# Products of zeros that warm TensorE: 256 columns instead of 512, twice as many

## The chip, the core and the metric

The kernel runs on one core of a Trainium2 chip. The metric is the device time of one execution in microseconds; lower is better. The core has five engines with a queue of instructions each: PE (TensorE, matrix products, with its weight loads shown apart as PEld), DVE (VectorE), ACT (ScalarE), POOL (GpSimd) and SP (SyncE, which only issues transfers here). An engine takes its instructions in the order in which they were written and waits where an operand is not there yet.

## The reference

An attention layer whose keys and values are first mixed block by block with a balanced 8x8 matrix for each of 32 heads, and then a feed-forward layer with the gate h * cos(h). Batch 4, 8 heads, 768 positions, head width 64, 8 blocks of 96; model width 512, inner width 2048.

```python
P = sort_net
for _ in range(5):                                # the balancing
    P = P - np.max(P, axis=-1, keepdims=True)
    P = np.exp(P)
    P = P / (np.sum(P, axis=-1, keepdims=True) + 1e-09)
    P = P / (np.sum(P, axis=-2, keepdims=True) + 1e-09)
k_sorted = np.einsum('bhij,bhjcd->bhicd', P, k_b)
v_sorted = np.einsum('bhij,bhjcd->bhicd', P, v_b)
scores = scale * np.matmul(q_b, k_sb.transpose(0, 1, 2, 4, 3))
attn = softmax(scores)
x = attn @ v_sb                                   # heads side by side: 3072 x 512
h = x @ w_in
out = (h * np.cos(h)) @ w_out
```

## The kernel before

The whole order of work is written out by hand (`tc.manual_schedule()`: nothing is moved by a scheduler). The kernel has three parts.

**Head.** At the start a 128x128 tile `warm` is filled with zeros on DVE (L231), and `keep_warm` (L244 to L248) multiplies it by its own first column, repeated over `cols` columns. The result goes to a PSUM tile that nobody reads: such a product of zeros only keeps TensorE at work. 14 of them, 512 columns each, run while the first loads arrive.

**Balancing.** `rounds(it)`, called five times, does the balancing of all 32 matrices in 32 partitions: one exponential on ACT (L335) and six operations on DVE (`normalize`, L309 to L314) in each round, every one of them waiting for the one before. Beside this chain the other engines prepare: POOL clears tiles and issues loads, PE transposes the first queries (`q_twice`, L323, 16 transposes in each of four calls) and ACT places them in SBUF (`q_place`, L329). The PSUM tiles of `q_twice` come from a pool of two, so its third call must wait for the first `q_place`, its fourth for the second. Between these calls `idle(times)` puts more products of zeros on PE: 4 after the first two calls of `q_twice` in round 0, 2 after the third and 2 after the fourth, in round 3. `idle` calls `keep_warm` with 512 columns. PE's written order up to the end of the balancing is therefore: 14 products of zeros; `q_twice(0)`, `q_twice(1)`; 4 products of zeros; `q_twice(2)`; 2; `q_twice(3)`; 2; and then `block` (L386), which needs the finished balanced matrix `sorted_by` (written by DVE in L314), the picking matrix in `pair` and a PSUM tile that `q_place(2)` has left.

**The rest.** `block` spreads the balanced matrix over 128 partitions, `spread` (L393, DVE) masks it, `kp` and `ks` (L408) sort the keys with it, `v0` (L785) the values, and the scores (L804), the softmax and the feed-forward layer (up products L860 and L672, cosine L676, gate L680, down products L697 and L881) follow, in eight groups of 384 positions. There are other products of zeros in this part (`fill=` in `s_ps`, `v0`, `p_ps`, `av_products`), with 512 columns in some calls and 256 in others; they are given straight to `keep_warm`.

Of the kernel before, what the change touches and what calls it, by code (L numbers as in the profile page):

```python
# [10 lines left out]
FP32 = mybir.dt.float32  # L11
# [7 lines left out]
def kernel(  # L19
# [46 lines left out]
    big = ctx.enter_context(tc.tile_pool(name="big", bufs=3, space=bass.MemoryType.PSUM))  # L66
# [177 lines left out]
    def keep_warm(times, t, cols=512):  # L244
        for _ in range(times):
            nc.tensor.matmul(
                t[:, :cols], warm[:], warm[:, :1].to_broadcast([128, cols]),
                start=True, stop=True)  # L248

    keep_warm(14, big.tile([128, 512], FP32, name="idle", tag="big"))  # L250


    V, A = nc.vector, nc.scalar
# [75 lines left out]
        A.copy(dst[:, h2], turns.pop(h2).rearrange("d e i r p -> d e i (r p)"))  # L329

    def idle(times):
        keep_warm(times, big.tile([128, 512], FP32, name="idle", tag="big"))

    def rounds(it):
        nc.scalar.activation(E, less[:], AF.Exp)  # L335
        if it == 0:
            A.copy(
                order.rearrange("k (p r) -> k p r", r=QR),
                ident[:blk, :blk].rearrange("k (r p) -> k p r", r=QR))
            q_twice(0)  # L340
            q_twice(1)
            idle(4)
        if it == 3:
            q_place(0)
            q_twice(2)
            idle(2)
            q_place(1)
            q_twice(3)
            idle(2)
# [905 lines left out]
```

## Time and profile before

| what | value |
|---|---|
| time, median of 3 runs | 232.1 us (231.99 to 232.11) |
| the profiled execution's own time | 231.61 us |
| its span, first to last instruction | 229.8 us |
| so outside the span | 1.8 us |
| PE products in the span | 2245 |
| products of zeros on the tile `idle` that the trace recorded | 21 of 22, first at 1.0 us, last at 11.0 us |

A row of a timeline gives the start in us from the span's beginning, the length, the engine, the line, what is written and read, the shape and the count; in brackets how long the engine had been idle just before and what ended the idle time. The length of a row of several products reaches from the first start to the last end. Products are pipelined: one lasts longer than the distance from its start to the start of the next, and it is this distance, the spacing, that a row of products costs. It is (length of the row - length of one product) / (count - 1). A few products are missing from the trace, so counts are now and then one short.

### The profile page before, as it was taken

The numbers are of one execution on the slowest core, as the hardware profiler recorded it, in microseconds if no ns is written. First come the engines' busy times: TensorE is split into PE (matmuls) and PEld (weight loads), VectorE is DVE, ScalarE is ACT, GpSimd is POOL, SyncE is SP. The second block draws the span as 40 slices with busy tenths as digits, with TensorE's granted clock in tenths as the row PEclk, the third lists the DMA queues.
The fourth block names the chain that finished last, engine by engine and source line by source line (L and its number), as shares of the span: only waits on it lengthen the run. The fifth ranks groups of instructions, "written<-read, shape, count | busy, mean of one in ns | idle before, by whom it ended". The sixth has DMA issues, their size and how long they took to land.

```text
span 229.8 us, 5513 instructions
## 1 busy us (share of the span) xinstructions
PE 220.8 (96%) x2245; PEld 138.7 (60%) x2268; DVE 170.8 (74%) x291; ACT 154.4 (67%) x207; POOL 96.1 (42%) x121
## 2 busy tenths in 40 slices
PE   8788999999999999999999999999999999999994
PEld 3378898567765566655665456655655565556554
DVE  6769968978698778868489977987699769646700
ACT  5659877777889858797688466736674667716521
POOL 7999999399950197943609000800000000000000
PEclk9999999999999999999999999999999999999999
DMA  6999999994999799667979939964924440351012
GB/s 83 225 187 207 202 206 236 195 227 148 124 124 191 171 139 148 118 135 146 162 118 163 135 74 148 210 98 81 206 92 80 90 160 0 69 147 46 0 46 94
DMA packets 67833, 31.21 MB, mean 136 GB/s; under 512 B 56416, under 2 KB 63200, under 8 KB 67552
## 3 DMA queue, kind: packets, MB, share of 16 engines
q0 software_dynamic: 24048, 13.64, 43.3%
q1 hardware_dynamic: 43472, 17.02, 35.1%
q8 instruction: 18, 0.29, 0.5%
q10 hardware_dynamic: 288, 0.20, 0.3%
q14 instruction: 7, 0.06, 0.1%
HBM read 27.27 MB, written 6.29 MB: 146 GB/s over the span
## 4 chain that ended last, share of the span: by engine, by line
PE 90%; DVE 3%; POOL 2%; issue 1%; ACT 1%; POOLq 0%; ACTq 0%
PE h L672 32%; PE o L697 30%; PE h L860 5%; PE o L881 4%; PE av L628 4%; PE sc L441 3%; PE ks L408 2%; PE o L1219 2%; PE pps L838 1%; PE sc L507 1%; PE xps L659 1%; PE vs L785 1%; PE vs L452 1%; PE qps L268 1%; PE xps L847 1%
## 5 line engine op out<-in xcount | busy, mean ns | idle before, releaser
L672 PE MATMUL h<-xT,w_in_t 128*128 128x384 bf16 x448 | 78.4, 326 | 0.1
L697 PE MATMUL o<-w_out_t,gg 128*128 128x512 bf16 x303 | 73.7, 379 | 1.0 <-issue 0.3
L676 ACT ACTIVATE c<-h,half_pi 128x768 f32<-128x768 f32 x56 | 50.5, 902 | 26.0 <-PE h L672 25.0
L680 DVE TENSOR_TENSOR gg<-c,h 128x768 bf16<-128x768 f32 x56 | 52.7, 949 | 19.5 <-ACT c L676 19.5
L672 PEld LDWEIGHTS <-w_in_t 128*128 128x128 bf16 x448 | 42.2, 98 | 26.3 <-DVE xT L259 0.6
L697 PEld LDWEIGHTS <-gg 128*128 128x128 bf16 x320 | 29.0, 99 | 28.3
L573 ACT ACTIVATE p_buf<-s 96x768 bf16<-96x768 f32 x32 | 26.6, 843 | 5.2 <-DVE s L494 4.0
L179 POOL COPY vperm<-kv 64x768 bf16<-64x768 bf16 (+2 forms) x12 | 28.4, 2416 | 3.9 <-DMA kv<-in_v_dram 3.9
L494 DVE TENSOR_TENSOR s<-sc,mx 96x384 f32<-96x384 f32 (+1 forms) x33 | 24.3, 735 | 1.6
L492 DVE TENSOR_REDUCE mx<-sc 96x4 f32<-96x384 f32 (+1 forms) x33 | 24.0, 729 | 0.2 <-PE sc L507 0.2
L641 DVE TENSOR_TENSOR xn<-av,r 96x512 bf16<-96x512 f32 x32 | 22.0, 687 | 1.1
L129 POOL DMA_DIRECT2D kv<-in_q_dram x24 | 16.0, 676 | 0.7 <-issue 0.7
L257 ACT COPY kv<-o 128x512 f32<-128x512 f32 (+2 forms) x10 | 5.2, 524 | 14.1 <-PE o L697 11.5
L257 ACT CAST kTs<-ks 128x512 bf16<-128x512 f32 (+1 forms) x18 | 11.0, 630 | 5.3 <-PE ks L408 4.4
L639 DVE RECIPROCAL r<-av 96x8 f32<-96x8 f32 x32 | 6.4, 199 | 9.6 <-PE av L628 9.1
L129 POOL DMA_DIRECT2D q_mem<-in_q_dram x16 | 10.7, 687 | 2.0 <-DMA kv<-in_v_dram 1.5
L881 PE MATMUL o<-w_out_t,gg 128*128 128x512 bf16 x45 | 11.2, 379 | 0.2
L259 DVE COPY kv<-o 128x512 f32<-128x512 f32 (+1 forms) x5 | 3.1, 612 | 11.1 <-PE o L1219 8.5
L860 PE MATMUL h<-xT,w_in_t 128*128 128x192 bf16 x128 | 11.1, 246 | 0.0
L441 PE MATMUL sc<-kTs,q_turned 128*128 128x96 bf16 x152 | 11.1, 206 | 0.0
L599 POOL CAST held<-q_turned 96x1 f32<-96x1 bf16 x2 | 0.4, 184 | 24.3 <-DMA q_turned<-q_mem 16.3
L860 PEld LDWEIGHTS <-w_in_t 128*128 128x128 bf16 x128 | 10.5, 98 | 0.0
(134 smaller groups left out, 285.6 us busy)
## 6 DMA issues: line engine op xcount, KB each, us to landing
out_dram<-kv SPq DMA_DIRECT2D x12, 256.0 KB, 2.7
out_dram<-o_s SPq DMA_DIRECT2D x10, 256.0 KB, 3.5
w_in_t<-in_moe_w_in_dram POOLq DMA_DIRECT2D x4, 512.0 KB, 11.7
w_out_t<-in_moe_w_out_dram POOLq DMA_DIRECT2D x4, 512.0 KB, 12.3
kv<-in_k_dram POOLq DMA_DIRECT2D x2, 768.0 KB, 9.8
kv<-in_v_dram POOLq DMA_DIRECT2D x2, 768.0 KB, 12.9
pair<-in_k_dram POOLq DMA_DIRECT2D x2, 768.0 KB, 12.3
kv<-in_v_dram POOLq DMA_DIRECT2D x6, 256.0 KB, 5.3
```

The lines of the kernel that those rows point to most:

```text
L129: nc.gpsimd.dma_start(out=q_heads[:, i, :, e], in_=src[:, ih * IC + i, :, e])
L179: nc.gpsimd.tensor_copy(dst, src)
L492: nc.vector.reduce_max(mx[:], scv, axis=AX.X)
L494: nc.vector.tensor_tensor(s, scv, mx.to_broadcast(list(s.shape)), op=ALU.subtract)
L573: nc.scalar.activation(p[:, :, :blk], s_t.pop((n, u)).rearrange("p e h c -> p (e h) c"), AF.Exp, scale=scale)
L641: nc.vector.tensor_tensor(xn.rearrange("p h e d -> p e h d"), avv[:, :, :, :D], r.to_broadcast([blk, 2, H2, D]), op=ALU.mult)
L672: nc.tensor.matmul(h[:, f2, :w], w_in_t[:, kk, f * 128:(f + 1) * 128], xT[n][:, kk], start=(kk == 0), stop=(kk == KC - 1))
L676: nc.scalar.activation(c[:], h[:, :, :w], AF.Sin, bias=half_pi[:, 0:1])
L680: nc.vector.tensor_tensor(gt[n, fp // 2][:, f:f + 2], c[:], h[:, :, :w], op=ALU.mult)
L697: nc.tensor.matmul(o[:], gt[n, f // 4][:, f % 4, ts * 128:(ts + 1) * 128], w_out_t[:, f, :], start=(f == 0), stop=(f == FC - 1))
L860: nc.tensor.matmul(o[:, part, f2 * w:(f2 + 1) * w], w_in_t[:, kk, f * 128:(f + 1) * 128], xT[0][:, kk, h * w:(h + 1) * w], start=(kk == 0) ...
L881: nc.tensor.matmul(out_ps[ts][:], gt[0, q][:, f % 4, ts * 128:(ts + 1) * 128], w_out_t[:, f, :], start=(f == 0), stop=(f == FC - 1))
```

## The change

Two calls of `keep_warm` ask for 256 columns and for twice as many products: at the head 28 instead of 14, and in `idle` 8, 4 and 4 instead of 4, 2 and 2. The number of columns stays 7168 at the head and 4096 beside the balancing. The other calls of `keep_warm` stay as they are.

```diff
-    keep_warm(14, big.tile([128, 512], FP32, name="idle", tag="big"))
+    keep_warm(28, big.tile([128, 512], FP32, name="idle", tag="big"), 256)
...
     def idle(times):
-        keep_warm(times, big.tile([128, 512], FP32, name="idle", tag="big"))
+        keep_warm(2 * times, big.tile([128, 512], FP32, name="idle", tag="big"), 256)
```

Every product brings its own weight load. On PE the end of the head reads as follows before, with the last products of zeros ahead of the first transpose (`q_mem` holds the queries as loaded, `qps` their transposes):

```order
L246 LDWEIGHTS warm
L246 MATMUL idle<-warm 128x512
L246 LDWEIGHTS warm
L246 MATMUL idle<-warm 128x512
L323 LDWEIGHTS q_mem [waits DMASW0_49]
L323 MATMUL qps<-ident,q_mem 64x4x24 [waits Pool_49]
```

And now:

```order
L246 LDWEIGHTS warm
L246 MATMUL idle<-warm 128x256
L246 LDWEIGHTS warm
L246 MATMUL idle<-warm 128x256
L246 LDWEIGHTS warm
L246 MATMUL idle<-warm 128x256
L246 LDWEIGHTS warm
L246 MATMUL idle<-warm 128x256
L323 LDWEIGHTS q_mem [waits DMASW0_49]
L323 MATMUL qps<-ident,q_mem 64x4x24 [waits Pool_49]
```

Nothing was moved; the transpose still waits for the load of the queries alone, and stands 28 rows later in PE's order. The second place on PE is the end of the balancing, where the last call of `idle` stands ahead of `block` (`pair` is the picking matrix). Before:

```order
L246 LDWEIGHTS warm
L246 MATMUL idle<-warm 128x512
L246 LDWEIGHTS warm
L246 MATMUL idle<-warm 128x512
L386 LDWEIGHTS pair [waits DVE_49,Pool_49]
L386 MATMUL bl<-sorted_by,pair 128x8 [waits Activation_49]
```

And now:

```order
L246 LDWEIGHTS warm
L246 MATMUL idle<-warm 128x256
L246 LDWEIGHTS warm
L246 MATMUL idle<-warm 128x256
L246 LDWEIGHTS warm
L246 MATMUL idle<-warm 128x256
L246 LDWEIGHTS warm
L246 MATMUL idle<-warm 128x256
L386 LDWEIGHTS pair [waits DVE_49,Pool_49]
L386 MATMUL bl<-sorted_by,pair 128x8 [waits Activation_49]
```

`block` waits for the same three engines as before. From here on every instruction of PE stands 44 rows later (22 products and their 22 weight loads), 4582 rows in all instead of 4538. The orders of ACT and SP are the same word for word, and on DVE and POOL only numbers of tiles differ.

## The prediction

> **What bounds the kernel now.** I read the page first, then the chain of waits over the first 15 us, then PE's timeline and its weight loads over the same stretch, because all 22 products that the change touches lie between 1.0 and 11.4 us. The page's engine row and its row of shares of the chain that ended last:
>
> ```profile
> span 229.8 us, 5513 instructions
> ...
> PE 220.8 (96%) x2245; PEld 138.7 (60%) x2268; DVE 170.8 (74%) x291; ACT 154.4 (67%) x207; POOL 96.1 (42%) x121
> ...
> PE 90%; DVE 3%; POOL 2%; issue 1%; ACT 1%; POOLq 0%; ACTq 0%
> ```
>
> PE carries 90% of the chain over the whole kernel, so one could think that any product more or less on PE is felt. For the stage at hand that is not so. This is PE's timeline there:
>
> ```profile
> 1.00 5.16 PE L246 MATMUL idle<-warm 128*128 128x512 bf16 x14 [1.00 <-DVE warm L231]
> 6.47 0.87 PE L323 MATMUL qps<-ident,q_mem 96*64 96x96 bf16 x32 [0.31 <-DMA q_mem<-in_q_dram]
> 7.28 0.82 PE L246 MATMUL idle<-warm 128*128 128x512 bf16 x3
> 9.33 0.53 PE L323 MATMUL qps<-ident,q_mem 96*64 96x96 bf16 x16 [1.23 <-ACT q_turned L329]
> 9.79 0.61 PE L246 MATMUL idle<-warm 128*128 128x512 bf16 x2
> 10.33 0.53 PE L323 MATMUL qps<-ident,q_mem 96*64 96x96 bf16 x16
> 10.79 0.61 PE L246 MATMUL idle<-warm 128*128 128x512 bf16 x2
> 12.08 0.35 PE L386 MATMUL bl<-sorted_by,pair 32*128 32x8 bf16 x8 [0.69 <-POOL held L368]
> ```
>
> The reader is to see the brackets. PE stands idle after the head's 14 products (0.31 us, until the queries land), after the next 4 (1.23 us, until ACT has emptied a PSUM tile) and after the last 2 (0.69 us). What PE waits for at 12.08 is seen in DVE's timeline (first row) and in the chain of waits (the others):
>
> ```profile
> 11.72 0.21 DVE L314 TENSOR_TENSOR sorted_by<-Q,over 32x64 bf16<-32x64 f32 x1
> ...
> 8.17 1.73 POOL w_in_t L160 x3
> ...
> 10.47 1.38 POOL kv L372
> ...
> 11.90 0.19 POOL held L368
> 12.09 0.36 PE bl L386 x8
> ...
> 12.75 1.56 PE ks L408 x48
> ```
>
> DVE writes the balanced matrix until 11.72 + 0.21 = 11.93, and POOL ends its clearing at 10.47 + 1.38 = 11.85; PE's `bl` cannot start before 11.93. (The chain leads through `held`, a POOL instruction that starts at 11.90; `block` itself waits for the balanced matrix and POOL's clearing, so I take 11.93 as what binds.) Up to here the time is set by the balancing on DVE and ACT and by POOL's queue, and no product of zeros is in it.
>
> **The change, step by step.** *A product of 256 columns at the full pace.* The kernel has some already, and its rows give the price (in the lower two, from the view of one line, least, median and greatest length in ns):
>
> ```profile
> 25.67 0.39 PE L246 MATMUL av<-warm 128*128 128x256 bf16 x2
> ...
> L246 PE MATMUL idle<-warm x21: 378/389/634, 1.0 to 11.0; 128*128 128x512 bf16 x21
> ...
> L246 PE MATMUL av<-warm x2: 272/273/274, 25.7 to 25.8; 128*128 128x256 bf16 x2
> ```
>
> Two of them take 0.39 us, one lasts 0.273, so the spacing is 0.39 - 0.27 = 0.12 us (0.11 to 0.12 within the rounding). For 512 columns the row at 7.28 gives (0.82 - 0.38) / 2 = 0.22 us, or by the row at 9.79, 0.61 - 0.38 = 0.23. Two halves for one whole cost -0.01 to +0.02 us. The 8 products beside the balancing become 16: -0.08 to +0.16 us of PE time in all, at most 4 x 0.02 = 0.08 ahead of the wait of 1.23 and 2 x 0.02 = 0.04 ahead of the wait of 0.69. Both waits hide it. I take 0; if the cover were gone it would cost at most the 0.16.
>
> The Trainium skill's page "TensorE: Matmul & The Clock Gate", section "Back-to-back issue gap", speaks against the change: a fixed 2.5 ns comes with each product at the full clock. By it 22 more products would cost an estimated 22 x 2.5 = 55 ns; our rows cannot resolve that, and it would lie under the same waits.
>
> *The fourth `q_twice`*, at 10.33, is the one place where PE does not wait behind filler: it starts because the 2 products before it end. It moves by at most 0.04 us. Its reader on ACT is covered:
>
> ```profile
> 8.50 1.46 ACT L329 COPY q_turned<-qps 128x768 bf16<-128x768 bf16 x2
> 10.19 0.26 ACT L335 ACTIVATE E<-less 32x64 f32<-32x64 f32 x1 [0.22 <-DVE less L314]
> 10.35 1.46 ACT L329 COPY q_turned<-qps 128x768 bf16<-128x768 bf16 x2
> 13.41 0.59 ACT L257 CAST kTs<-ks 128x512 bf16<-128x512 f32 x1 [1.60 <-PE ks L408]
> ```
>
> The second copy of the pair at 10.35 starts about 11.1, after the transposes end at 10.33 + 0.53 = 10.86, and ACT is then idle for 1.60 us. So 0 again.
>
> *The head at the slow pace.* In the first microseconds the products come more slowly. The weight loads, one ahead of each product, show it:
>
> ```profile
> 4.39 0.15 PEld L246 LDWEIGHTS <-warm 128*128 128x128 bf16 x1 [0.28 <-issue]
> 4.82 0.15 PEld L246 LDWEIGHTS <-warm 128*128 128x128 bf16 x1 [0.28 <-issue]
> 5.13 0.54 PEld L246 LDWEIGHTS <-warm 128*128 128x128 bf16 x3 [0.17 <-issue]
> ```
>
> A load every 4.82 - 4.39 = 0.43 us, then, from 5.13 on, three in 0.54 us: the spacing halves to 0.22 at about 5.0 us, 4 us after the first product. The granted-clock column of the profile reads full speed all the while, so it is the spacing that tells. Each load takes 0.15 us and lies wholly within the product before it. No row shows 256 columns at the slow pace, so I bound them: half of 0.43, 0.21 us, if the load stays hidden (0.15 is less than 0.21); 0.15 + 0.21 = 0.36 if load and product came one after the other. At 0.21 the 28 products take the 4.0 us with 19 of them and the other 9 follow at 0.11: the last starts near 6.0 and the row ends near 6.2, as now. At 0.36, 11 go by until 5.0, and 17 at 0.12 take 2.0 us: the row ends near 7.2, `q_twice` would run 7.1 to 8.0 instead of 6.47 to 7.34, and the next filler, 8 at 0.12, until 9.1, still before PE's wait ends at 9.33. ACT takes the first of these tiles at 8.50, and it would be there by 7.6. So both ends give 0 on the path; I take the hidden load, since the rows show 0.15 of load under each product.
>
> *Sum.* Head 0, beside the balancing 0, transposes 0: **+0.0 us**. The profiled execution's own time, 231.6 (span 229.8 and 1.8 around it), stays 231.6; the median of the runs, 0.5 above it, stays **232.1 us**.
>
> **Rivals.** *1. The slow pace lasts (slower).* If whatever sets PE's pace took the shorter products for less work, the pace could still be halved when the balancing ends. Up to 9.33 us nothing would be late beyond the waits. It decides from 12.08 us on: the 48 products of `ks` take 1.56 us there and would take up to 3.1, and the products of zeros behind them, of which the code has 3 and the trace 2, 3 x 0.22 = 0.66 more:
>
> ```profile
> 14.78 0.81 PE L246 MATMUL sc<-warm 128*128 128x512 bf16 x2
> ...
> 15.96 0.95 DVE L824 TENSOR_REDUCE mx<-sc 96x8 f32<-96x768 f32 x1 [0.25 <-PE sc L804]
> ...
> 27.59 0.58 PE L860 MATMUL h<-xT,w_in_t 128*128 128x192 bf16 x5
> ```
>
> That is +1.6 to +2.2 us by 15.96, when DVE, idle for 0.25 us, gets the first scores, and nothing behind it gives the time back before PE's first up product at 27.59. I price it at +2.0: 233.6 own, 234.1 median. For it speaks that the pace did change once in this trace, after 4 us of products. Against it: the columns in a row are the same number, the bounds above leave no longer pause between products, and this trace stays at the full pace from 5.0 to 12.08 through pauses of 0.31, 1.23 and 0.69 us. The same page of the Trainium skill, section "Part 1: The HAM clock gate (the "warmup" mystery)", states that the pace follows a window of about 3.4 us in time and not a number of products; by that rule 28 halves do as well as 14 wholes, which the step at 5.0 us agrees with and does not prove.
>
> *2. PE's instructions stand elsewhere (either sign).* PE has one pause without a wait in the middle of a row of products:
>
> ```profile
> 17.96 0.26 PE L804 MATMUL sc<-kTs,q_turned 64*128 64x64 bf16 x5 [0.27 <-DVE s L828]
> 18.47 0.34 PE L804 MATMUL sc<-kTs,q_turned 64*128 64x64 bf16 x11 [0.26 <-issue]
> 19.20 0.61 ACT L257 CAST vS<-vs 96x512 bf16<-96x512 f32 x1 [0.15 <-PE vs L785]
> q8 instruction: 18, 0.29, 0.5%
> ```
>
> The trace gives no cause for the 0.26 us at 18.21. If it belongs to a place in the instruction stream (q8 brings the instructions in 18 pieces of 0.29 / 18 MB, 16 KB), 44 more rows put it 22 products earlier in the work: past these 5, past 8 of the values, into the ninth from the end of the scores before them, ahead of the place where PE waits 0.27 us for DVE anyway. Then between 0.15 (ACT's wait at 19.20) and 0.26 us is won: 231.8 to 232.0 median. It may as well fall on products for which ACT waits, and cost 0.26 more or, if the old pause stays and a new one comes, up to twice that: 232.4 to 232.6. The Trainium skill, "Runtime: NRT & Kernel Launch", section "Instruction fetch mechanics", has instructions refilled in blocks of 256, with the cost of a boundary mostly hidden; no run here shows that the pause is such a boundary.
>
> *3. The loads do not hide.* Worked out above as 0.36 us a product: PE ends the head 1 us later and the waits swallow it, so the time is 232.1 as well. It would show in the profile, not in the time.
>
> **How the numbers follow.** A measurement of this kernel can tell about 0.2%, 0.46 us, from no change. The forecast with rival 3, no change within 0.25 us: 0.78. The pause of rival 2 gained: 0.07, of which 0.04 might reach past 0.46 us together with what follows it. The pause lost: 0.09, of which 0.05 past 0.46. Rival 1: 0.06. To the forecast's share I add 0.02 on either side for what these 30 us of the trace do not show. That makes faster 0.04 + 0.02 = 0.06, slower 0.05 + 0.06 + 0.02 = 0.13 and the same 0.81. The range takes in the bounds of rival 2 on both sides with a little of what may follow: 231.5 to 232.8; rival 1 stays outside.
>
> **What the profile after would show.** Right: the last product of zeros of the head ends between 6.0 and 6.4 us, the first transpose is still released by the load of the queries near 6.5, `bl` starts at 12.0 to 12.1 with an idle time of 0.5 to 0.7 before it, and the 48 products of `ks` take 1.56 us. The hidden load: weight loads 0.21 us apart in the first 4 us; at 0.36 rival 3 is right. Rival 1: loads still 0.21 apart after 8 us, or `ks` above 2 us. Rival 2: the pause of 0.26 in the scores at 18 us gone or elsewhere, with PE's first up product moved by as much. I am wrong if `bl` starts later than 12.2, or if `bl` and the first up product stay where they are and the end of the kernel moves.

## The result, and the profile after

The change makes the kernel slower: 234.14 us (median of 6 runs, 233.71 to 235.82) against 232.11 us before (6 runs, 231.99 to 232.65), a ratio of 1.0095 with an interval of 1.0066 to 1.0124. The prediction was 232.1 us, no change, with a range that ended at 232.8. The profiled execution of the changed kernel is the longest of its six, 235.8 us of its own time. The page after:

```profile
span 234.0 us, 5558 instructions
...
PE 222.9 (95%) x2268; PEld 142.3 (61%) x2290; DVE 171.1 (73%) x291; ACT 154.1 (66%) x207; POOL 95.9 (41%) x121
...
PE 83%; DMA 9%; POOL 2%; ACT 2%; issue 2%; DVE 0%; SPq 0%; ACTq 0%; POOLq 0%
```

PE is busy 2.1 us longer (part of it at a lowered clock, below), but the row of shares has the news: a DMA share of 9% in a chain that had none worth naming before. PE's timeline over the head tells where it enters (start, length, then the idle time ahead of a row in brackets):

```profile
1.00 5.99 PE L246 MATMUL idle<-warm 128*128 128x256 bf16 x28 [1.00 <-DVE warm L231]
7.02 0.87 PE L323 MATMUL qps<-ident,q_mem 96*64 96x96 bf16 x32
...
9.48 0.53 PE L323 MATMUL qps<-ident,q_mem 96*64 96x96 bf16 x16 [0.59 <-ACT q_turned L329]
9.94 0.62 PE L246 MATMUL idle<-warm 128*128 128x256 bf16 x4
...
12.24 0.35 PE L386 MATMUL bl<-sorted_by,pair 32*128 32x8 bf16 x8 [0.67 <-POOL held L368]
12.91 1.56 PE L408 MATMUL ks<-bd,kv 128*128 128x64 bf16 x48 [0.31 <-DVE bd L393]
...
15.68 0.40 PE L804 MATMUL sc<-kTs,q_turned 64*128 64x64 bf16 x16
17.41 0.42 PE L785 MATMUL vs<-bdv,vperm 128*128 128x64 bf16 x8 [1.34 <-POOL vperm L179]
...
20.32 0.63 PE L785 MATMUL vs<-bdv,vperm 128*128 128x64 bf16 x8 [0.69 <-POOL vperm L179]
```

The stretch that the change touches does what was forecast. The halves fit beside the balancing (four of them take 0.62 us, the two wholes 0.61), PE still waits 0.67 us ahead of `bl`, and `ks` takes 1.56 us to the hundredth. `bl` starts 0.16 us later than before; the kernels below start it at 12.08 to 12.28, and one of them, `small`, at 12.26 and takes the same time as before (232.03), so I count that as scatter between executions. The first large loss comes behind all that, at 16.07 us: PE has the scores done and waits 1.34 us, and later 0.69 us, for POOL's copies of the values (`vperm`). Before, the same 8 products started with no wait:

```profile
15.85 0.42 PE L785 MATMUL vs<-bdv,vperm 128*128 128x64 bf16 x8
```

POOL's timeline, first of before, then of after:

```profile
13.94 5.87 POOL L179 COPY vperm<-kv 64x768 bf16<-64x768 bf16 x4 [0.36 <-DMA kv<-in_v_dram]
```

```profile
15.90 5.81 POOL L179 COPY vperm<-kv 64x768 bf16<-64x768 bf16 x4 [2.17 <-DMA kv<-in_v_dram]
```

The copies take as long as ever and start 1.96 us later, because the load of the values (768 KB) is late. It was issued at 2.7 us by POOL, in the same place of the same queue. The chain of waits of after goes through it:

```profile
2.72 13.13 DMA kv<-in_v_dram
...
15.90 4.37 POOL vperm L179 x3
...
20.32 0.63 PE vs L785 x8
```

What else moved? The DMA view, cut to 13.5 to 14.9 us, lists what the transfer engines carried there (packets, MB, share). Before:

```profile
q0 software_dynamic: 287, 0.29, 125.6%
```

After:

```profile
q0 software_dynamic: 263, 0.27, 114.4%
q8 instruction: 1, 0.02, 4.4%
```

A 16-KB piece of instructions (q8) now travels there. It is the first of the 18; before, it travelled at 16 us, as the same view of before over 15.9 to 17.1 us shows:

```profile
q0 software_dynamic: 233, 0.24, 119.5%
q8 instruction: 1, 0.02, 5.1%
```

The records of single packets and of the semaphore that POOL waits for show the collision (read from the packed trace; a completion write is a packet of 4 bytes, 16 of them for this load, as many as there are transfer engines):

```
us from the span's start             before          after
last data packet ends                13.36           13.84
completion writes, first to last     12.88 - 13.36   15 of them by 13.84, the 16th 14.79 - 14.81
last of the semaphore's 16 updates   13.89           15.85
POOL's first copy starts             13.94           15.90
first piece of instructions travels  16.04 - 17.02   13.82 - 14.80
```

The records do not name the engine of a packet; that the piece is on the engine of the 16th write is read from their times. Before, the last write starts 0.02 us before the last data packet ends (13.34 against 13.36). After, the piece starts at that place (13.82 against 13.84), and the write follows 0.02 us before the piece ends. So on one engine the piece of instructions goes in between the load's last data and its completion write. It takes 0.98 us. POOL starts 0.05 us behind the 16th update in both kernels, so the load has landed only when all 16 are there. Put in order of time, the first 15 updates stand 0.5 to 0.7 us behind the writes, the last 1.04 us; why the last takes longer the trace does not show.

The second loss stands near the end of the kernel. PE's timeline there, before:

```profile
204.79 1.03 PE L697 MATMUL o<-w_out_t,gg 128*128 128x512 bf16 x4
205.66 5.53 PE L672 MATMUL h<-xT,w_in_t 128*128 128x384 bf16 x33
```

and after:

```profile
207.74 1.03 PE L697 MATMUL o<-w_out_t,gg 128*128 128x512 bf16 x4
209.86 3.41 PE L672 MATMUL h<-xT,w_in_t 128*128 128x384 bf16 x20 [1.09 <-DMA xT<-xn]
```

A wait of 1.09 us for the transposes `xT` is new. The DMA view over 197 to 212 us gives their median time from issue to landing, before and then after:

```profile
xT<-xn SPq DMA_TRANSPOSE x3, 2.3
```

```profile
xT<-xn SPq DMA_TRANSPOSE x3, 4.3
```

The 17th piece of instructions travels at 206.7 us before and at 204.3 after; with the 2.95 us by which all work is later there (207.74 - 204.79), that is 5.3 us earlier in the work, among these transposes. The waits of PE in sum, by the list of waits of after:

```profile
PE vs L785 <- POOL vperm L179: 2.0, 2, 1.3
PE h L672 <- DMA xT<-xn: 1.1, 1, 1.1
```

The third loss is part of the first and not in every execution. The windows of after (start and end, length, busy time of PE, PEld, DVE, ACT, POOL, then the granted clock, DMA share, GB/s):

```profile
18.00:20.00 2.00, 1.62 (x47) 1.31 (x45) 1.13 (x3) 1.73 (x4) 2.00 (x2) 1.00 1.24 206
20.00:22.00 2.00, 1.69 (x30) 1.55 (x31) 1.97 (x3) 1.67 (x3) 2.00 (x3) 0.59 1.24 208
22.00:24.00 2.00, 1.78 (x16) 1.45 (x16) 1.57 (x2) 0.92 (x2) 2.00 (x4) 0.56 1.29 201
```

After the wait of 1.34 us the granted clock falls to half for 3.41 us (20.34 to 23.76 by the clock's own records). The row at 20.32 shows it: 8 products of the values take 0.63 us instead of 0.42. Two of the six runs have a mean clock under 1, the profiled one (235.82) and one of 234.74; the other four, at 1.000, lie at 233.71 to 234.19. So the stretch at half clock costs some 0.5 to 2 us where it comes, by these runs, and the median's 2.0 us is nearly all lost without it.

The profiled execution adds up. PE's first up product starts at 30.17 us instead of 27.59, +2.58, which holds the late values and the half clock. The shift stays 2.58 until 147 us, grows to 2.95 by 158 us and to 4.20 behind the wait for `xT`: the whole difference of the spans, 234.0 - 229.8. The part behind the first up product is thus 1.6 us here, and 1.0 us in the profile of `again` below (4.4 - 3.4). Of the 2.0 us that the four runs at full clock lose, an estimated 0.4 to 1.0 us are then the head's, and half or more comes later.

### The profile page after: what moved, and what is told of

It is laid out like the page before. It is cut to its first block, busy times and chain, and to the rows that moved or that the text cites. A ratio compares the mean times of both kernels' runs of the same rounds, so it can differ in the third digit from the quotient of the medians.

```text
span 234.0 us, 5558 instructions
## 1 busy us (share of the span) xinstructions
PE 222.9 (95%) x2268; PEld 142.3 (61%) x2290; DVE 171.1 (73%) x291; ACT 154.1 (66%) x207; POOL 95.9 (41%) x121
## 3 DMA queue, kind: packets, MB, share of 16 engines
q1 hardware_dynamic: 43472, 17.02, 34.3%
## 4 chain that ended last, share of the span: by engine, by line
PE 83%; DMA 9%; POOL 2%; ACT 2%; issue 2%; DVE 0%; SPq 0%; ACTq 0%; POOLq 0%
PE h L672 31%; PE o L697 25%; DMA kv<-in_v_dram 6%; PE h L860 5%; PE o L881 4%; PE av L628 4%; PE sc L441 2%; DMA vperm<-p_buf 2%; POOL vperm L179 2%; PE o L1219 2%; PE ks L408 1%; DMA xT<-xn 1%; PE vs L785 1%; PE pps L838 1%; PE sc L507 1%
## 5 line engine op out<-in xcount | busy, mean ns | idle before, releaser
L129 POOL DMA_DIRECT2D kv<-in_q_dram x24 | 15.9, 675 | 0.8 <-issue 0.8
L257 ACT CAST vS<-vs 96x512 bf16<-96x512 f32 x16 | 9.1, 583 | 3.0 <-PE vs L785 2.9
```

The costliest lines, as they stand in the source:

```text
L129: nc.gpsimd.dma_start(out=q_heads[:, i, :, e], in_=src[:, ih * IC + i, :, e])
L257: eng.copy(dst, src)
```

## The experiments

Two theories stood at the start, and the expectations name them by letter. **F**: the 44 more rows of PE's order (22 products and 22 weight loads) move the pieces of instructions, and what these collide with pays; the width of a product does not matter. **H**: the products of 256 columns themselves are to blame, by the pace or the clock that PE keeps, and the pieces only happen to lie elsewhere. F1 to F5 are forms of F that the expectations state as they come up; by F3 the first piece can't travel before the first load of the up weights has ended. Ratios are against the kernel before on the same chip (its medians lay between 231.9 and 232.2 us).

**again**: the changed kernel once more.

> The changed kernel once more. What is to be seen first is whether its profile shows the same two things as the first one: the load of the values landing about 1.5 us later than before (POOL's first copy of vperm near 15.9 instead of 13.9 us), and the first piece of PE's instructions brought near 13.8 instead of 16.0 us, that is in the tail of that load. Theory F (fetch): yes to both, 234 us. Rival H (the halves themselves, by the pace of TensorE or by their own cost): 234 us, with the place of the fetch of no meaning.

Measured: 234.09 us, ratio 1.0101 (1.0057 to 1.0145). The result stands; the piece of instructions travels at 13.7 us, POOL waits 2.1 us for the values, PE 0.7 for `xT`.

**rows44**: before, with 22 products of 8 columns behind the first call of `idle`; 44 more rows, and not one product of 256 columns that wasn't there.

```
+        t = big.tile([128, 512], FP32, name="idle", tag="big")
+        keep_warm(times, t)
+        if times == 4:
+            keep_warm(22, t, 8)
-        keep_warm(times, big.tile([128, 512], FP32, name="idle", tag="big"))
```

> Before, with its products of 512 columns, and 22 more products of zeros with 8 columns each behind the first call of idle, where PE waits 1.23 us for ACT (22 x 0.026 = 0.6 us fits in). PE's order grows by the same 44 rows as in the change, without a product of 256 columns. F: the fetch moves as in the change, 234.1 us. H: 232.1 us.

Measured: 234.45 us, 1.0091 (1.0064 to 1.0118). POOL's and PE's timelines (lines stand 3 lower in this kernel):

```profile
15.75 5.84 POOL L179 COPY vperm<-kv 64x768 bf16<-64x768 bf16 x4 [2.03 <-DMA kv<-in_v_dram]
```

```profile
17.28 0.42 PE L788 MATMUL vs<-bdv,vperm 128*128 128x64 bf16 x8 [1.21 <-POOL vperm L179]
```

The same waits at the same places: the rows cost it, not the columns.

**head_only** and **idle_only**: the two parts of the change alone, 28 and 16 more rows.

```
 head_only
-    keep_warm(14, big.tile([128, 512], FP32, name="idle", tag="big"))
+    keep_warm(28, big.tile([128, 512], FP32, name="idle", tag="big"), 256)
 idle_only
-        keep_warm(times, big.tile([128, 512], FP32, name="idle", tag="big"))
+        keep_warm(2 * times, big.tile([128, 512], FP32, name="idle", tag="big"), 256)
```

> Only the head has 28 products of 256 columns, idle as before: 28 more rows on PE. By F the first fetch is asked for when PE's instructions have been taken up to about row 363; with 28 more rows this place lies behind a wait of the first scores for DVE (about 15.5 us), so the fetch stays behind the load of the values: 232.1 us. H: 14 of the 22 new products, so 14/22 of 2.0, 233.4 us.

> Only idle has twice as many products of 256 columns, the head as before: 16 more rows on PE. F: 232.1 us, as for the head alone, with the first fetch at 15.5 us or later. H: 8 of the 22 new products, 0.7 us, 232.8 us.

Measured: head_only 233.74 us, 1.0069 (1.0048 to 1.0091); idle_only 232.6 us, 1.003 (1.0012 to 1.0048). Both numbers are nearer to H, and F's were missed. But the profiles show neither a lowered pace at `ks` nor a late load of the values. In head_only PE's timeline has a pause in the middle of the scores, with no wait that the profile can name:

```profile
18.81 0.18 PE L804 MATMUL sc<-kTs,q_turned 64*128 64x48 bf16 x1 [1.31 <-issue]
```

So F, as it stood, lacked a second way to pay: where the first piece is not moved, PE runs out of instructions. Whether the 256 columns had a part was open, and the next run is made for that.

**rows28**: as rows44, with 14 products of 8 columns instead of 22, the 28 rows of head_only without its halves.

```
-            keep_warm(22, t, 8)
+            keep_warm(14, t, 8)
```

> Before with 14 tiny products (8 columns) behind the first call of idle: the 28 more rows of the head alone, but no product of 256 columns. F2: as the head alone, fetch near 16.4, a pause of about 1.3 us near row 445, 233.7 us. H: 232.1.

Measured: 233.49 us, 1.0077 (1.0049 to 1.0106), as head_only, and the same pause:

```profile
18.53 0.18 PE L807 MATMUL sc<-kTs,q_turned 64*128 64x48 bf16 x1 [1.07 <-issue]
```

H falls. The pause stands at row 445 to 447 of PE's own order in every kernel that has it, before included (its 0.26 us at 18.21), wherever that row lies in the work: the traces record 222 or 223 weight loads ahead of it. In the eight profiles that have it, PE goes on 1.23 to 1.45 us behind the end of the first piece's transfer (17.02 and 18.47 before, 17.24 and 18.53 here). So the first of the 18 pieces is needed there.

**same_rows** and **no_idle**: no more rows than before, by leaving out products of zeros beside the balancing (all 8 in both); the head has 22 products of 256 columns in same_rows, its 14 of 512 in no_idle.

```
 same_rows
-    keep_warm(14, big.tile([128, 512], FP32, name="idle", tag="big"))
+    keep_warm(22, big.tile([128, 512], FP32, name="idle", tag="big"), 256)
 both
-        keep_warm(times, big.tile([128, 512], FP32, name="idle", tag="big"))
+        pass
```

> 22 products of 256 columns at the head and none beside the balancing: as many products and rows on PE as before, so every later instruction stands where it stood, with half the columns of zeros. F2: fetch near 16.0 and the pause of about 0.3 us near row 445 as before, 232.1 us, if TensorE keeps its pace without the products beside the balancing. H: half the columns in products that cost more: above 232.5. If the pace falls for want of those products, key products of 3 us instead of 1.56 show it.

> Before without the 8 products of 512 columns beside the balancing (14 at the head stay): 16 rows fewer on PE. F2: the place where PE's old instructions end comes 8 products later in the work, and PE reaches it about 0.2 us later, so the pause of 0.26 us shrinks: 231.8 to 232.1 us. A rival by which those products keep the pace up: above 233, with key products slower than 1.56 us.

Measured: same_rows 233.66 us, 1.0074 (1.005 to 1.0098); no_idle 234.87 us, 1.0119 (1.0085 to 1.0152). Both are slow for a reason of their own: without the products beside the balancing the clock falls, as the windows and PE's timeline of same_rows show.

```profile
10.00:12.00 2.00, 0.88 (x17) 0.66 (x15) 1.41 (x8) 1.76 (x4) 1.96 (x2) 0.50 0.93 197
```

```profile
12.93 2.72 PE L408 MATMUL ks<-bd,kv 128*128 128x64 bf16 x48 [0.31 <-DVE bd L393]
```

As a test of the rows these runs are inconclusive. They do show two things: neither has the wait for `xT`, and what the prediction's rival 1 would have looked like (2.72 us for `ks`), which the changed kernel does not have.

**hold**: the change, with one product of 8 columns that reads the first turned keys, put ahead of the second block of `kp`, to keep PE, and the request for the piece with it, back.

```
+        if t == 1:
+            nc.tensor.matmul(
+                o[:, 0, :8], warm[:], kT[0][:, 0, IC, 32:40], start=True, stop=True)
```

> The changed kernel, with one product of 8 columns more, ahead of the third group of key products, that reads a piece of kTs which ACT writes until about 14.1 us: PE's instructions are held there until the load of the values has landed, and only then the first piece of instructions is asked for. Theory F2 (the 44 rows bring the fetch forward into the tail of the load of the values; the fetch itself takes about 2.3 us until PE goes on, and PE pauses where its old instructions end if the fetch was asked for late): the values land near 13.8, the fetch starts near 14.2 instead of 13.7, POOL's copy starts near 14.3 instead of 15.9, and there is no pause near PE's row 445: 231.6 to 232.2 us, although all 44 products of 256 columns are there. Theory F1 (44 more rows cost by themselves): 234. Rival H (products of 256 columns cost): 234.

Measured: 233.23 us, 1.0067 (1.0044 to 1.0091). A miss: the piece travelled at 13.3 us, before the product held PE (14.0 to 14.2 us), so the hold came too late to tell anything. PE's wait for the values was 0.47 us here.

**small**, **after_small**, **rows28_small**: before, the change and rows28, with the load of the up weights cut into 256, 512, 640 and 640 columns instead of four times 512, so that its first part ends earlier.

```
-        c = slice(z * Dff // 4, (z + 1) * Dff // 4)
+        c = slice((0, 256, 768, 1408)[z], (256, 768, 1408, 2048)[z])
```

> Before with the shorter first load of w_in alone. F3: fetch near 14.9 instead of 16.0, the pause of 0.26 us at PE's row 445 goes: 231.6 to 231.9 us. If the pause has another cause: 232.0 or above.

> The change with the shorter first load of w_in. F3: there the fetch is asked for early enough to go in at the end of the load of the values, ahead of its completion, which the size of the next load does not alter: the values land near 14.7 as in the change, 234.0 us. If the change cost what rows28 costs (a pause of PE for late instructions): 232.

> As rows28 (28 more rows, no product of 256 columns), but the four loads of w_in are cut at 256, 768 and 1408 columns instead of at each 512, so that the first is half as long. Theory F3: a piece of instructions is taken by its transfer engine only where a load ends on it; in rows28 it stood behind the first load of w_in (2.5 us) and PE paused 1.3 us for it. With the half as long first load the fetch starts near 15.0 instead of 16.3, the pause goes: 231.7 to 232.3 us. A theory by which 28 more rows cost by themselves: 233.5.

Measured: small 232.03 us, 0.9996 (0.9987 to 1.0005); after_small 234.52, 1.0112 (1.007 to 1.0155); rows28_small 233.8, 1.0081 (1.0057 to 1.0105). The first pieces start at 16.4, 13.7 and 16.4 us, and the pauses and waits stay. F3 falls: the first load of the up weights lands at 15.49 us in small instead of 16.25, and the first piece starts at 16.38 instead of 16.04, so the end of that load is not what it waits for.

**late_v**: before, with four clearings of a buffer on POOL ahead of its first copy of the values. No row of PE is added; the copies are as late as after the change.

```
+    for _ in range(4):
+        zero_words(nc.gpsimd, p_bufs[2].rearrange("p a c -> p (a c)"))
```

> Before with four clearings of an unused tile on POOL ahead of its first copy of the values, 4 x 0.48 = 1.9 us: the copy starts near 15.6 instead of 13.9, as the change's does through the late load, with the instructions where they were. If the late copy is what the change costs: 233.5 to 234.2 us. If POOL's copy has time to spare: 232.1.

Measured: 234.57 us (233.27 to 235.05), 1.0097 (1.0069 to 1.0124). POOL's timeline, PE's, and one of the windows:

```profile
13.54 2.30 POOL L197 MEMSET p_buf<- 96x512 f32 x4
15.79 5.79 POOL L179 COPY vperm<-kv 64x768 bf16<-64x768 bf16 x4
```

```profile
17.30 0.64 PE L785 MATMUL vs<-bdv,vperm 128*128 128x64 bf16 x8 [1.39 <-POOL vperm L179]
```

```profile
18.00:20.00 2.00, 2.00 (x44) 1.74 (x44) 0.71 (x1) 1.31 (x3) 2.00 (x2) 0.50 1.24 206
```

Late copies alone give PE the same wait (1.39 us) and a like loss, with the half clock in all four runs. There is no wait for `xT` and the 17th piece is where it was. What late copies cost without the half clock no run shows by itself; nearest is hold, whose copies start at 15.41 us at full clock and whose first up product starts 1.06 us later than before, with the 0.37 us in it by which its own product delays `ks`.

**behind**: the 44 rows put in front of the first scores, behind the place where, by the theory of the time (F4), PE asks for the first piece (25 products of 8 columns instead of 3 of 512).

```
-        keep_warm(fill, o[:, 0])
+        keep_warm(25 if fill else 0, o[:, 0], 8)
```

> Before, with 25 products of 8 columns in place of the 3 products of 512 columns ahead of the first scores (25 x 0.026 = 0.65 us, as long as the 3): 44 more rows on PE, but behind the balancing and the key products instead of ahead of them, and no product of 256 columns. Theory F4: PE asks for a piece of instructions when it takes an instruction near its row 202, 240 rows ahead of the place near row 446 where that piece begins. Here the asking is not moved, so the fetch stays near 16.0 us and the values land on time, but row 446 holds work that PE reaches 1 us sooner: a pause of about 1.2 us near row 446, 233.2 to 233.7 us. A theory by which the rows cost only through the late values: 232.0.

Measured: 233.84 us, 1.0081 (1.0057 to 1.0105). The piece travels at 16.0 us as before, the values are on time (POOL's copy starts at 14.23), and PE runs dry at row 447 instead:

```profile
18.26 0.38 PE L804 MATMUL sc<-kTs,q_turned 64*128 64x48 bf16 x9 [0.96 <-issue]
```

So 44 rows at this place leave the first piece where it was, unlike 44 rows beside the balancing, and the loss is the pause instead of late values.

**rows36**: rows44 with 18 products instead of 22, in a single run.

```
-            keep_warm(22, t, 8)
+            keep_warm(18, t, 8)
```

> Before with 18 products of 8 columns behind the first call of idle: 36 more rows, so that PE's wait for the balanced matrix stands at its row 209, between those of rows28 (201, fetch near 16.3) and of rows44 (217, fetch near 13.7). F4 with row 202: the asking comes ahead of that wait, fetch near 13.7 us, POOL's copy near 15.8, no pause near row 446, about 234 us. If the place lies at 210 to 217: fetch near 16.3 us, copy near 14.2, a pause of over 1 us, about 233.6 us.

Measured: 233.1 us. F4's time for the piece came out, its late values and its 234 us did not: the piece travels at 13.6 us, as early as after the change, but it starts at 13.59 us, with the load's last completion write (13.58 to 13.60). The values are on time and PE has no pause. This run parts an early piece from late values, and does so by luck. POOL's timeline, then PE's near the end:

```profile
14.26 5.85 POOL L179 COPY vperm<-kv 64x768 bf16<-64x768 bf16 x4 [0.55 <-DMA kv<-in_v_dram]
```

```profile
207.12 3.09 PE L675 MATMUL h<-xT,w_in_t 128*128 128x384 bf16 x18 [0.97 <-DMA xT<-xn]
```

The first up product starts at 27.70 us, 0.11 later than before: the head's loss is gone. What is left, 1.1 us against 231.96, lies behind it, most of it at the wait of 0.97 for `xT`; profile against profile, the work is 0.2 us later from 155 us on and another 1.1 behind this wait.

**late_rows**: before, with 22 products of 8 columns near 159 us, behind the head and ahead of the 17th piece.

```
+    keep_warm(22, big.tile([128, 512], FP32, name="idle", tag="big"), 8)
```

> Before with 22 products of 8 columns ahead of the up products of the sixth group (near 159 us), where PE is the bound: they cost 22 x 0.026 = 0.6 us of PE themselves and put 44 rows behind the head, which stays as it was. Theory F5: the change loses a second time near 205 us, because the next to last fetch falls 4 to 5 us earlier in the work (201 to 203 instead of 206.5 us), among the transfers that transpose the last xT, and PE's up products wait for xT. Then 0.6 and 0.7 to 1.2 us: 233.2 to 233.8 us, with that wait in the profile. If the late wait came from the head (whatever is late there): 0.6 alone, 232.6 us, no wait for xT.

Measured: 233.59 us, 1.0064 (1.0046 to 1.0082). PE's timeline has the added products and, 47 us later, the wait:

```profile
159.93 0.69 PE L246 MATMUL idle<-warm 128*128 128x8 bf16 x22
...
207.12 3.08 PE L672 MATMUL h<-xT,w_in_t 128*128 128x384 bf16 x18 [0.47 <-DMA xT<-xn]
```

The 17th piece has moved from 206.7 to 202.9 us while the head is untouched: the second loss needs nothing of the first. The added products themselves are in the 1.4 us too.

All together (medians in us; "rows" are those added ahead of the first scores; the other columns are read from one profile each):

```
kernel       rows       median  1st piece  POOL waits  PE pause   17th piece  PE waits
                                at         for values  near 446   at          for xT
before       0          232.1   16.0       0.4         0.3        206.7       -
small        0          232.0   16.4       0.7         0.4        207.1       -
late_v       0          234.6   15.7       - (busy)    -          208.1       -
same_rows    0          233.7   16.2       0.8         -          208.3       -
no_idle      -16        234.9   16.4       0.8         -          209.6       -
idle_only    16         232.6   16.0       0.5         0.4        203.1       0.5
rows28       28         233.5   16.3       0.6         1.1        203.6       0.7
head_only    28         233.7   16.4       0.5         1.3        205.0       0.5
rows28_small 28         233.8   16.4       0.4         1.3        205.6       0.8
behind       44 behind  233.8   16.0       0.5         1.0        203.3       0.8
late_rows    44 late    233.6   16.3       0.4         0.4        202.9       0.5
rows36       36         233.1   13.6       0.6         -          202.7       1.0
after        44         234.1   13.8       2.2         -          204.3       1.1
again        44         234.1   13.7       2.1         -          205.2       0.7
rows44       44         234.5   13.7       2.0         -          204.9       0.7
after_small  44         234.5   13.7       2.0         -          205.3       0.9
hold         46         233.2   13.3       1.7         -          202.9       0.8
```

The last column splits without an exception: the twelve runs with more rows wait for `xT`, the five without do not. The transposes themselves show why. The 17 profiles have 221 of them for `xT`, from issue to landing: of the 163 with no piece travelling in the 2.3 us behind the issue, 158 take 2.28 to 2.41 us (the other five stand near 205 to 207 us behind delayed ones); the 58 with a piece take 2.60 to 4.86 us. That holds before too, where a piece at 155.6 us meets two of them (3.60 and 2.97 us) and PE does not wait.

## Why the prediction was wrong

**The products themselves: right.** Two halves cost what one whole does (0.62 against 0.61 us above), and the waits beside the balancing hide what little there is (0.59 of the 1.23 us are left ahead of the second transposes, 0.67 of 0.69 ahead of `bl`). rows44 and rows28 bring the loss without a single half. Rival 3 did not occur either: the head's 28 weight loads take 5.68 us, 0.21 apart and not 0.36. The head's last product ended at 6.99 us, not 6.0 to 6.4: the step to the full pace came at 6.7 us in this execution instead of 5.0. The first transpose started 0.55 later, and the wait behind it took that up, as the prediction argued for its slower bound. `bl` starts at 12.24 us, past the prediction's mark of 12.2, but so does small's (12.26), which loses nothing.

**Rival 1: right in number, absent in fact.** It priced a lasting slow pace at 234.1 us. The median is that, but `ks` takes 1.56 us, the mark that the prediction set for it. Only the pace in same_rows and no_idle (`ks` 2.72) is that rival.

**The step that failed is the size of rival 2.** The sum has no term for the 44 rows; they stand in that rival alone, as a pause gained (0.07) or lost (0.09). The prediction saw the pause of 0.26 us, saw the 18 pieces on q8, and reckoned that 44 rows put a piece's boundary elsewhere. It then priced that as a pause of PE alone: 0.26 us once more, "up to twice that", 232.4 to 232.6, and let the range end at 232.8. The runs show three prices in place of one. *A pause is not 0.26 us*: with 28 rows it is 1.07 to 1.34 us, since the piece does not come sooner when PE needs it sooner. *A piece is a transfer*, and delays another one when it moves: in the changed kernel the last completion write of the load of the values comes 1.45 us later, its landing and POOL's copies 1.96 later, and PE waits 1.34 + 0.69. *All 18 pieces move*, not the first: the 17th falls among the transposes of `xT` and costs PE 0.5 to 1.1 us, and idle_only, with 16 rows and an untouched head, loses 0.3% to it. The prediction's own test for this rival was the first up product and the pause; its last sentence (the head stays and the end moves) named the late part as a way to be wrong, without a price.

That the pause belongs to a place in the instruction stream, open before, is shown now by its row. The Trainium skill, "Runtime: NRT & Kernel Launch", section "Instruction fetch mechanics", has the refills in 16-KB blocks and the cost of a boundary mostly hidden. The trace agrees on the 16 KB; on "hidden" the runs decide against it here, with 0.26 to 1.34 us for a late piece and 0.5 to 2.0 for a piece in another's way.

**The clock.** The prediction looked for a lower clock where the products are shorter; it came where PE waits, in some executions only. The Trainium skill's page "TensorE: Matmul & The Clock Gate", section "Part 1: The HAM clock gate (the "warmup" mystery)", gives a free-running window of about 3.4 us and two states, half and full speed. The stretches at half clock agree: 3.41 us in the changed kernel's profile, 6.83 in that of `again`, and 3.41 or 6.83 in the others that have one.

**Still open.** When a piece is asked for is in no record. Where it travels jumps: at 15.7 to 16.4 us with up to 28 rows ahead of the scores and at 13.3 to 13.8 with 36 to 46, with nothing between, and why is not known. Of the growth by 0.37 us near 155 us I can say only this: the two transposes of `vperm` take 4.58 and 3.56 us there instead of 2.78 and 2.79 and PE waits 0.20 us for them, by the waits of after,

```profile
PE av L628 <- DMA vperm<-p_buf: 0.2, 1, 0.2
```

and the 14th piece travels 3.0 us earlier in the work (155.2 - 2.58 against 155.6 us). That is the same pattern a third time. No run was made for it, but the ten profiles with 28 or more rows ahead of that place lose 0.1 to 0.4 us there, and idle_only (16 rows) and the kernels without more rows lose nothing. No version beat the kernel before; small equals it.

## What to carry to other kernels

A change of the number of instructions is a change of the times at which later instructions are fetched, and each fetch is a 16-KB transfer on an engine that loads use too: before predicting "hidden by a wait", look where every piece of the instruction queue travels and which loads or transposes end there. Give such a rival the price of a late load at each of these places, not that of one pause. To test whether a change works by what it computes or by where it puts instructions, add the same number of the smallest instructions in its place.

## What the runs showed of the hardware

Instruction pieces share the transfer engines with loads, and one of 0.98 us can stand between a load's last data and its completion write: 15 writes were done at 13.84 us and the sixteenth at 14.81. A piece that travels while a transpose of `xT` is under way stretches it from 2.3 to between 2.6 and 4.9 us in these profiles. 22 products of 8 columns near 159 us, 0.69 us of work, delay transposes 47 us later (2.3 us before, 3.7 with them). And products of zeros can be needed just where they look idle: without the eight beside the balancing (same_rows) the granted clock was 0.50 from 10.0 to 16.8 us and `ks` took 2.72 us instead of 1.56.
